# Chunk 0's k and q as bf16 over the software queue, chunk 2's x turned by the DMA engines: a fused window attention and MLP kernel

## The chip, the core and the metric

The kernel runs on one core of one Trainium2 chip. The metric is the device time of one execution in microseconds (us); the number shown is the median of three runs. The engines are named as in the profile: PE is TensorE's matmul side and PEld its weight loads, DVE is VectorE, ACT ScalarE, POOL GpSimd, SP SyncE. POOL, SP and ACT can all issue DMAs. Those of POOL go through the software queue (q0 in the profile), which can change the type on the way; those of SP and ACT go through hardware queues (q1 and q10), which cannot, but which can transpose bf16 data. All share 16 DMA engines.

## The reference

Inputs are q, k and v of shape (4, 8, 768, 64) in fp32 (batch, heads, tokens, head size). Each query attends to the 128 latest keys and to the first 4 of its sequence; the result goes through a normalised MLP with a residual.

```python
scores = scale * np.matmul(q, k.transpose(0, 1, 3, 2))
keep = is_sink | in_window            # first 4 keys, or 0 <= i - j < 128
a = softmax(where(keep, scores, -1e9))
x = (a @ v)                           # heads side by side: (4, 768, 512)
xn = (x - mu) / np.sqrt(var + 1e-06) * g_ln
out = x + np.maximum(xn @ w_ch1, 0.0) @ w_ch2     # w_ch1 512 x 2048, w_ch2 2048 x 512
```

## The kernel before, in words

**Tiling.** The 4 x 768 tokens are 24 tiles of 128, or 12 chunks of 256; a sequence has three chunks. Chunks 0 to 2 are the first sequence. For each chunk, `chunk(c)` (L642) loads k, q and v and turns k and q so that the head size lies along the partitions; `attend_tile(t)` (L724, chunks 0 and 1), `attend(c)` (L784, chunk 2) or `block(t)` (L902, all later ones) computes scores, exponents and the product with v; `normalise` (L865) takes the mean and variance of x and subtracts the mean (tile `xc`); and `mlp(c)` (L1015) does the two big products. The second product's result is scaled by the inverse deviation when the residual is added (L1070), and stored by SP (L1074).

**Order.** The program has no loops at run time over this: each piece of work is an operation (`P.op`) with the engines that may do it, an estimated duration, a priority, and the buffers it reads and writes. `Plan.run` (L114) places them, before the program is built, on a model of the engines, of PSUM and SBUF slots and of the DMA engines, each engine taking among the operations that could start about now the one with the lowest priority number. The instructions are then written out in the order of the planned start, engine by engine; on the chip each engine works through its list in that order. A load's plan entry has three numbers: the time it keeps the DMA engines, the delay to its first byte, and the delay after its last. In the gaps that the plan shows on TensorE in the first 24 us, matmuls on a zeroed tile are put in (L1132).

**k and q of chunk 0 (L647 to L676).** They come in quarters: k and q, each in two halves of four heads. SP issues k's halves and ACT q's (L656), in fp32, into tile `natf`; a row of a partition holds two neighbouring tokens (i = 0, 1) of each head, so that one run of memory is 512 bytes. ACT or DVE casts each quarter to bf16 (L660, `natc`). Four matmuls against the identity turn it (L668): each has 128 partitions and two heads of 64 columns, and writes into a PSUM tile `one`, even tokens for i = 0 and odd ones for i = 1. One eviction of 512 columns (L639) copies it to `kT` or `qT`. `tile_of` notes which eviction the scores of a tile wait for: here one for both tiles.

**k and q of chunks 1 to 3 (`by_pairs`, L575).** POOL loads all eight heads in one load that casts to bf16 (L581, `natp`). Quarter matmuls of 64 partitions by 64 columns turn them (L596), and evictions (L639) put the tokens of each tile in order. From chunk 4 on (`by_dma=4`) k and q are loaded by POOL (L692, `nat`) and transposed by DMAs that SP issues (L573).

**x of a tile (L880 to L898).** For chunks below `x_by_dma` (3 before) TensorE transposes the four blocks of `xc` (L885), and an eviction (L896, DVE) multiplies by `g_ln` (tile `gt`) on the way to `xnt`, what the first product reads. From chunk `x_by_dma` on, SP issues a DMA transpose (L573 through `dma_t`), and `g_ln` must sit in w1 instead:

```python
        if c == PAR["x_by_dma"] - 1:
            for s in range(4):
                for j in range(NDM):
                    P.op(f"w1g{s}{j}", {"DVE": fix(0.26)}, 16.0 * c + 11.0 + 2 * s + 0.1 * j,
                         ... V.tensor_scalar_mul(w1[s][:, j, :], w1[s][:, j, :], gt[:, j:j + 1]) ...
                         reads=[Bw1[s], Bc["gt"]], writes=[Bw1g[s]], after=last_use[s])
```

So each of the four quarters of w1 is scaled in place on the DVE (L1096), once its last matmuls with the unscaled weights are done, and the first product of chunk `x_by_dma` waits for it.

**Other loads.** v of each tile (L616, later L634), w1 in four loads (L547) and w2 in four (L550) come through POOL, cast to bf16. The other set-up work: POOL makes the identity and the triangle mask (L467, L470), the DVE the masks and ones (L463 to L523), SP loads `gt` (L525) and the first four keys' v (L529).

**A second path.** If a sum of exponents is out of range, `general` (L236) computes everything again; it does not run here.

Of the kernel before, what the change touches and what calls it, by code (L numbers as in the profile page):

```python
# [65 lines left out]
class Plan:  # L66
# [47 lines left out]
    def run(self):  # L114
        free = {"PE": 0.9, "ACT": 0.75, "DVE": 0.9, "POOL": 1.3, "SP": 0.75}
# [81 lines left out]
def pe(us):  # L197
    return {"PE": (us, us + Plan.PE_DRAIN)}
# [17 lines left out]
HW_V = (0.2, 0.8, 1.2)  # L216
SW_P = (1.47, 0.7, 0.9)
# [14 lines left out]
PAR = dict(strict=400.0, win=0.4, tr=-8.0, sc=-5.0, sc1=-2.0, av=2.0, blk=-8.0, step=6.0, trx=9.0, by_dma=4, x_by_dma=3,  # L232
# [136 lines left out]
def kernel(  # L369
# [43 lines left out]
    ring("natc", 4, [128, 2, 4, 64], BF16)  # L413
# [197 lines left out]

    def load_v(t, prio):
        b, r = t // RB, t % RB
        bv = Buf(f"v{t}", "vn")
        vn_b[t] = bv
        P.op(f"vld{t}", {"POOL": (0.87, 0.9)}, prio, lambda e: G.dma_start(  # L616
            bv.t[:, :, 0:64], v[b, :, 128 * r:128 * (r + 1), :].rearrange("h p d -> p h d")),
            writes=[bv], dma=SW, after=list(ones_of.values()))
# [23 lines left out]
    def chunk(c):  # L642
# [3 lines left out]
        if c < 2:  # L646
            kT_b[c], qT_b[c] = Buf(f"kT{c}", "kT"), Buf(f"qT{c}", "qT")  # L647
            if c == 0:
                nats = [Buf("kf", "natf"), Buf("qf", "natf")]
                for hh in range(2):  # L650
                    hs = slice(4 * hh, 4 * hh + 4)
                    for i, (x, T) in enumerate(((k, kT_b[c]), (q, qT_b[c]))):
                        nm, src, part = "kq"[i], nats[i], Buf(f"{'kq'[i]}l{hh}")
                        ap = x[b, hs, 0:256, :].rearrange("h (p i) d -> p h (i d)", i=2)
                        P.op(f"{nm}ld{hh}", {("SP" if i == 0 else "ACT"): (0.53, 0.53)}, -70 + hh,
                             lambda e, src=src, ap=ap, hs=hs: (nc.sync if e == "SP" else nc.scalar).dma_start(  # L656
                                 src.t[:, hs].rearrange("p h i d -> p h (i d)"), ap), writes=[src, part], dma=HW_F)
                        nat, pt, done = Buf(f"{nm}c{hh}", "natc"), Buf(f"pt{nm}{hh}", "one"), Buf(f"{nm}T0{hh}")
                        P.op(f"cast{nm}{hh}", {"DVE": dve(512), "ACT": act(512)}, d + 0.01 * hh,
                             lambda e, nat=nat, src=src, hs=hs: (nc.scalar.copy if e == "ACT" else V.tensor_copy)(  # L660
                                 nat.t, src.t[:, hs].rearrange("p h i d -> p i h d")),
                             reads=[part], hold=[src], writes=[nat])

                        def tr(e, pt=pt, nat=nat):
                            pb = pt.t.rearrange("p (h m i) -> p h m i", h=2, i=2)
                            for hp in range(2):
                                for i in range(2):
                                    nc.tensor.matmul(pb[:, hp, :, i], lhsT=nat.t[:, i, 2 * hp:2 * hp + 2, :], rhs=ident,  # L668
                                                     start=hp + i == 0, stop=True, skip_group_check=True)
                        o = P.op(f"tr{nm}{hh}", pe(0.3), d + 0.02 + 0.01 * hh, tr, reads=[nat, Bc["ident"]], hold=[T], writes=[pt])  # L670
                        trs[0], trs[1] = trs.get(0, [o]), [o]
                        evict(f"ev{nm}0{hh}", d + 0.05 + 0.01 * hh, 512,
                              lambda pt=pt: pt.t.rearrange("p (h c) -> p h c", h=2),
                              lambda T=T, hh=hh: T.t[:, 2 * hh:2 * hh + 2, :], [pt], [T, done], fp=True)
                        for t in range(2):
                            tile_of[nm, t, hh] = done  # L676
# [499 lines left out]
```

## Time and profile before

| | us |
|---|---|
| median of the runs shown (3; 217.49 to 218.28) | 217.88 |
| the profiled execution | 219.3 |
| its span, first to last instruction | 217.8 |
| PE busy | 207.1 (95%) |
| DVE busy | 117.7 (54%) |
| ACT busy | 106.1 (49%) |
| POOL busy | 111.7 (51%) |
| mean granted TensorE clock (share of full) | 0.995 |

| DMA queue | packets | MB |
|---|---|---|
| software (q0) | 69872 | 13.18 |
| hardware, SP (q1) | 33024 | 13.61 |
| hardware, ACT (q10) | 1056 | 0.52 |

How to read it: the busy time of an engine is an average over stages. The kernel has a start of some 23 us, in which the first loads come and the attention of the first four tiles goes through all engines, and then eleven stretches of some 16 us, one to a chunk, in which TensorE has work all the time. In the views below, times in us run from the first instruction of the span. A line of the timeline has start, duration, engine, source line, operation, output and inputs, sizes, the number of instructions merged, and in brackets how long the engine sat idle before and what ended that. A line of the chain has start, duration and what it was. The packet records of the trace give each DMA packet's queue, size and time, and the landing records the time at which a load's semaphore was complete.

### The profile page before, as it was taken

How to read it: one execution, taken by the hardware profiler on the slowest of the kernel's cores; microseconds unless marked ns; L12 is line 12 of the kernel's file. 1: busy time of each engine (PE TensorE's matmuls, PEld its weight loads, DVE VectorE, ACT ScalarE, POOL GpSimd, SP SyncE). 2: the span in 40 equal slices, each digit the busy share in tenths (PEclk: the TensorE clock that was granted, in tenths of full speed). 3: DMA queues.
4: the chain of work that ended last, by engine and by line, in shares of the span. 5: the costliest groups of instructions: out<-in, count | busy, mean ns of one | idle time of the engine just before them, and what ended most of it. 6: DMA issues, size and time to landing. Idle time of an engine off the chain costs nothing.

```text
span 217.8 us, 6716 instructions
## 1 busy us (share of the span) xinstructions
PE 207.1 (95%) x2774; PEld 145.3 (67%) x2797; DVE 117.7 (54%) x324; ACT 106.1 (49%) x171; POOL 111.7 (51%) x166
## 2 busy tenths in 40 slices
PE   6979999999999999999999999999999999999991
PEld 2657975765875875864865865865865866856760
DVE  5389874696986447446355456355366266262021
ACT  3687477155572562562562562552652652622600
POOL 7877642589961881871970980970960120120000
PEclk9999999999999999999999999999999999999998
DMA  5999999999999699799799799799999202203011
GB/s 155 171 188 204 194 206 193 181 132 136 204 161 125 115 127 146 83 194 147 110 148 139 110 137 157 107 142 144 113 142 138 75 1 74 72 7 116 0 54 60
DMA packets 103990, 27.82 MB, mean 128 GB/s; under 512 B 94224, under 2 KB 101008, under 8 KB 103952
## 3 DMA queue, kind: packets, MB, share of 16 engines
q0 software_dynamic: 69872, 13.18, 80.7%
q1 hardware_dynamic: 33024, 13.61, 32.5%
q10 hardware_dynamic: 1056, 0.52, 0.9%
q8 instruction: 24, 0.39, 0.8%
q14 instruction: 14, 0.11, 0.2%
HBM read 27.43 MB, written 6.29 MB: 155 GB/s over the span
## 4 chain that ended last, share of the span: by engine, by line
PE 90%; DVE 5%; issue 2%; ACT 1%; DVEq 0%
PE one L1062 38%; PE one L1033 35%; PE pair L967 3%; PE one L1026 2%; PE one L940 2%; PE pair L1132 2%; PE one L947 2%; DVE x L860 1%; PE one L956 1%; DVE st L868 1%; PE one L668 1%; PE one L975 1%; PE pair L740 1%; DVE xnt L896 1%; PE pair L596 1%
## 5 line engine op out<-in xcount | busy, mean ns | idle before, releaser
L1062 PE MATMUL one<-w,h 128*128 128x512 bf16 (+1 forms) x377 | 84.8, 370 | 2.3 <-issue 1.6
L1043 ACT ACTIVATE h<-one 128x512 bf16<-128x512 f32 x94 | 56.2, 598 | 48.6 <-PE one L1033 44.9
L1033 PE MATMUL one<-xnt,w 128*128 128x256 bf16 x704 | 79.5, 273 | 0.0
L1033 PEld LDWEIGHTS <-w 128*128 128x128 bf16 x704 | 68.5, 98 | 10.6 <-issue 0.3
L1062 PEld LDWEIGHTS <-h 128*128 128x128 bf16 x400 | 37.2, 98 | 39.1
L985 ACT ACTIVATE pe<-pair 128x768 bf16<-128x768 f32 x36 | 27.2, 808 | 43.0 <-PE pair L967 43.0
L634 POOL DMA_DIRECT2D vn<-in_v_dram x59 | 38.7, 701 | 9.9 <-DMA w<-in_moe_w_ch_dram 6.5
L877 POOL TENSOR_SCALAR st<-st 128x1 f32<-128x1 f32 x24 | 8.7, 363 | 66.7 <-DVE st L870 66.3
L1008 DVE RECIPROCAL rec<-one 128x4 f32<-128x4 f32 x36 | 6.4, 177 | 57.0 <-PE one L956 45.6
L1070 DVE SCALAR_TENSOR_TENSOR ot<-one,st,x 128x512 f32<-128x512 f32 (+1 forms) x25 | 18.2, 727 | 14.0 <-PE one L1062 9.3
L878 POOL TENSOR_TENSOR st<-st,mhalf 128x1 f32<-128x1 f32 x24 | 16.9, 703 | 2.0
L868 DVE BATCH_NORM_STATS2 st<-x 128x6 f32<-128x512 bf16 x24 | 16.7, 695 | 0.8
L1010 DVE TENSOR_TENSOR x<-one,rec 128x256 bf16<-128x256 f32 x36 | 15.3, 424 | 1.2
L692 POOL DMA_DIRECT2D nat<-in_k_dram x16 | 14.9, 939 | 1.1 <-DMA natp<-in_q_dram 1.1
L692 POOL DMA_DIRECT2D nat<-in_q_dram x16 | 14.3, 908 | 0.0
L990 DVE TENSOR_TENSOR pe<-pe,band 128x768 bf16<-128x768 bf16 x24 | 12.2, 551 | 0.0
L872 DVE TENSOR_SCALAR xc<-x,st 128x512 bf16<-128x512 bf16 x24 | 9.1, 381 | 1.1 <-DVE st L870 0.3
L967 PE MATMUL pair<-qT,kT 64*64 64x128 bf16 (+1 forms) x528 | 9.2, 204 | 0.0
L940 PEld LDWEIGHTS <-pe 128*128 128x128 bf16 (+1 forms) x144 | 6.2, 97 | 2.9 <-issue 0.8
L765 ACT ACTIVATE pe<-pair 128x1024 bf16<-128x1024 f32 (+1 forms) x8 | 7.1, 918 | 2.0 <-PE pair L759 1.0
L1026 PE MATMUL one<-xnt,w 128*128 128x128 bf16 x128 | 7.6, 219 | 0.0
L967 PEld LDWEIGHTS <-kT 64*64 64x64 bf16 x528 | 7.2, 108 | 0.4 <-issue 0.4
(106 smaller groups left out, 165.2 us busy)
## 6 DMA issues: line engine op xcount, KB each, us to landing
out_dram<-ot SPq DMA_DIRECT2D x23, 256.0 KB
w<-in_moe_w_ch_dram POOLq DMA_DIRECT2D x8, 512.0 KB, 14.2
nat<-in_k_dram POOLq DMA_DIRECT2D x16, 128.0 KB, 4.8
nat<-in_q_dram POOLq DMA_DIRECT2D x16, 128.0 KB, 5.5
vn<-in_v_dram POOLq DMA_DIRECT2D x44, 32.0 KB, 5.5
vn<-in_v_dram POOLq DMA_DIRECT2D x15, 64.0 KB, 5.1
natp<-in_k_dram POOLq DMA_DIRECT2D x3, 256.0 KB, 13.8
vn<-in_v_dram POOLq DMA_DIRECT2D x6, 128.0 KB, 11.8
```

The source lines that it names most:

```text
L634: P.op(f"vld{t}_{i}", {"POOL": (0.8, 0.85)}, prio + 0.001 * i, lambda e, p0=p0, n=n, hs=hs, src=src: G.dma_start(m.t[p0:p0 + n, hs, 0:64], ...
L692: lambda e, nat=nat, ap=ap: G.dma_start(nat.t, ap), writes=[nat], dma=SW, after=gate(c))
L868: P.op(f"bn{t}", {"DVE": fix(0.60)}, d + 0.12, lambda e: V.bn_stats(st.t[:, 8:14], x.t), reads=[x], writes=[st, mv])
L878: G.tensor_tensor(st.t[:, 16:17], st.t[:, 17:18], mhalf, op=ALU.pow)),
L967: nc.tensor.matmul(pps[u].t[64 * g:64 * g + 64, h2, col + c0:col + c0 + n], lhsT=kt.t[rs, hp, k0:k0 + 64], rhs=qT.t[rs, hp, q0:q0 + n], st ...
L985: nc.scalar.activation(pes[j].t.rearrange("p a b -> p (a b)")[:, 0:768].rearrange("p (a b) -> p a b", a=2), pps[j].t[:, :, 0:384], AF.Exp, ...
L990: V.tensor_mul(at_s, at_s, band[j] if r > 1 else edge[r][j].unsqueeze(1).to_broadcast([128, 4, 192]))
L1010: P.op(f"x{t - 1}{u}", {"DVE": dve(256)}, d + 0.051 + 0.002 * u, lambda e, u=u, rc=rc, pv=pv: V.tensor_tensor(x.t[:, 256 * u:256 * u + 256 ...
L1033: nc.tensor.matmul(ph.t[:, 256 * s:256 * s + 256], lhsT=w1[ht // 4][:, j, 128 * (ht % 4):128 * (ht % 4 + 1)], rhs=xnt.t[:, j, :], start=j ...
L1043: nc.scalar.activation(hb.t, ph.t, AF.Relu)
L1062: nc.tensor.matmul(pc.t[:, 0:wd], lhsT=(h1[2 * s + i].t[:, 128 * ii:128 * ii + 128] if by_tile else h1[ht // 2].t[:, 256 * (ht % 2) + 128 ...
L1070: V.scalar_tensor_tensor(ot.t[:, sl], in0=pc.t[:, 0:wd], scalar=st.t[:, 16:17], in1=x.t[:, sl], op0=ALU.mult, op1=ALU.add),
```

## The change

Two things change, and three constants of the planner with them.

1. For chunk 0, the new function `by_halves` takes the place of the code at L649 to L676. POOL issues the four quarters of k and q, which are cast to bf16 on the way into `natc`; there is no cast on ACT or DVE, and SP and ACT issue none of these loads. Sixteen quarter matmuls of 64 by 64 turn each quarter into two PSUM tiles, one for each tile of tokens, and each has its own eviction of 256 columns. `tile_of` now names, for each tile, its own eviction; the second tile's has a priority number larger by 0.4. The loads' priorities put the first two ahead of the identity mask on POOL and the others around the triangle mask.
2. `x_by_dma` goes from 3 to 2: x of chunk 2 (tiles 4 and 5) is transposed by DMAs, and w1 is scaled by `g_ln` after chunk 1's first product instead of chunk 2's.

```diff
-        free = {"PE": 0.9, "ACT": 0.75, "DVE": 0.9, "POOL": 1.3, "SP": 0.75}
+        free = {"PE": 0.9, "ACT": 0.75, "DVE": 0.9, "POOL": 1.0, "SP": 0.75}
...
+SW_F = (0.74, 1.1, 0.9)
...
-... by_dma=4, x_by_dma=3,
+... by_dma=4, x_by_dma=2,
...
-    ring("natc", 4, [128, 2, 4, 64], BF16)
+    ring("natc", 4, [128, 4, 2, 64], BF16)
...
+    def by_halves(nm, src, T, hh, i, d):
+        nat = Buf(f"{nm}c{hh}", "natc")
+        ap = src[0, 4 * hh:4 * hh + 4, 0:256, :].rearrange("h (p i) d -> p h (i d)", i=2)
+        P.op(f"{nm}ld0{hh}", {"POOL": (0.6, 0.63)}, (-101.0, -100.0, -98.5, -97.0)[2 * hh + i], lambda e: G.dma_start(
+            nat.t.rearrange("p h i d -> p h (i d)"), ap), writes=[nat], dma=SW_F)
+        pts = [Buf(f"pt{nm}{hh}{r}", "one") for r in range(2)]
+
+        def tr(e):
+            for a in range(2):
+                for u in range(2):
+                    for h2 in range(2):
+                        for r in range(2):
+                            rs, cs = slice(64 * r, 64 * r + 64), slice(64 * h2, 64 * h2 + 64)
+                            pb = pts[r].t[:, 0:256].rearrange("p (h i m) -> p h i m", h=2, i=2)
+                            nc.tensor.matmul(pb[cs, a, u, :], lhsT=nat.t[rs, 2 * a + h2, u, :], rhs=ident[rs, rs],
+                                             start=True, stop=True, skip_group_check=True)
+        o = P.op(f"tr{nm}0{hh}", pe(0.3), d + 0.02 + 0.01 * hh, tr, reads=[nat, Bc["ident"]], hold=[T], writes=pts, mode="q")
+        trs[0], trs[1] = trs.get(0, [o]), [o]
+        for r in range(2):
+            done = Buf(f"{nm}T0{hh}{r}")
+            evict(f"ev{nm}0{hh}{r}", d + 0.05 + 0.01 * hh + 0.4 * r, 256,
+                  lambda r=r: pts[r].t[:, 0:256].rearrange("p (h i m) -> p h m i", h=2, i=2),
+                  lambda r=r: T.t[:, 2 * hh:2 * hh + 2, 128 * r:128 * r + 128].rearrange("p h (m i) -> p h m i", i=2),
+                  [pts[r]], [T, done], fp=True)
+            tile_of[nm, r, hh] = done
...
-                        P.op(f"{nm}ld{hh}", {("SP" if i == 0 else "ACT"): (0.53, 0.53)}, -70 + hh,
...
-                        P.op(f"cast{nm}{hh}", {"DVE": dve(512), "ACT": act(512)}, d + 0.01 * hh,
...
-                        evict(f"ev{nm}0{hh}", d + 0.05 + 0.01 * hh, 512,
...
+                        by_halves("kq"[i], x, T, hh, i, d)
```

24 lines of the change are left out of this document (1 added, 23 removed).

## The prediction

> **What bounds the kernel now.** I read the chain of work that ended last, first its shares and then its pieces in time, then the timeline of the first 24 us, then the busy times by stage.
>
> ```profile
> PE 90%; DVE 5%; issue 2%; ACT 1%; DVEq 0%
> ```
> ```profile
> 8.01 0.59 ACT qT L639
> ...
> 8.94 0.54 PE one L668 x4
> ...
> 12.11 0.19 DVE rec L858
> ...
> 47.18 0.22 PE one L885 x4
> ...
> 48.27 0.22 PE one L885 x4
> ...
> 55.19 6.99 PE one L1033 x64
> ```
>
> TensorE sets the end: from about 23 us on its pieces follow each other without a hole, so a microsecond saved there, or by which that dense stretch starts earlier, is a microsecond of the whole. The DVE's 5% lie before 23 us, where the chain goes through the attention of the first four tiles. The timeline shows what that stretch waits for:
>
> ```profile
> 1.02 1.01 SPq L656 DMA_DIRECT2D natf<-in_k_dram  x2
> ...
> 1.85 1.12 POOL L581 DMA_DIRECT2D natp<-in_k_dram  x1
> ...
> 7.25 0.43 DVE L660 CAST natc<-natf 128x512 bf16<-128x512 f32 x1 [0.30 <-DMA natf<-in_q_dram]
> ...
> 8.87 0.61 PE L668 MATMUL one<-ident,natc 128*128 128x128 bf16 x4
> ...
> 9.48 0.74 POOL L547 DMA_DIRECT2D w<-in_moe_w_ch_dram  x1 [0.42 <-DMA natp<-in_k_dram]
> 9.52 0.69 DVE L639 CAST qT<-one 128x512 bf16<-128x512 f32 x1 [1.84 <-PE one L668]
> ```
> ```profile
> 12.00:15.00 3.00, 2.44 (x81) 1.76 (x77) 2.71 (x7) 2.69 (x5) 2.64 (x3) 1.00 1.62 187
> ...
> 21.00:24.00 3.00, 2.93 (x58) 2.65 (x56) 2.90 (x9) 1.19 (x2) 2.17 (x3) 1.00 1.34 201
> ```
>
> The last quarter of k and q lands at 7.22, is cast until 7.68, turned at 8.87, evicted until 10.21, scored at 10.36; the first reciprocal of tile 0 starts at 12.11. By stage (window, length, then busy us of PE, PEld, DVE, ACT, POOL) the DVE is nearly full from 12 to 24 us: once it has work, it is the bound until TensorE takes over.
>
> **The change, first half: k and q of chunk 0.**
> *Landing.* Four issues move from SP and ACT to POOL. POOL is free at 1.1 (its sequencer waits from 1.08). Each has 512 packets; the nearest rows with 512 are v loads (0.77) and weight loads (0.74): 0.75 each, 0.12 more for the first (1.12 against 0.9 to 1.0 for later ones of its form), and two mask instructions of 0.29 between them: the last ends at 1.1+3.0+0.12+0.58=4.8. When the software queue is idle, its first packet comes 1.69 us after the issue starts, 0.71 after it ends (72.67 to 74.36, again at 88.91 and 104.79). It moves 71 packets of 256 B per 0.1 us (packet records, 7.1 to 7.5 us), 0.72 a load; landing comes about 1.1 after the last packet (66.86 to 68.12). So the first lands near 1.1+1.69+0.72+0.3 (slow start)+1.1=4.9 and the last near 4.8+0.71+0.72+1.1=7.3. Before it was 4.86 and 7.22: nothing won or lost here. SP and ACT lose two issues of 0.5 each; what stood behind them, gt (used at 15.7) and the table load, is early anyway. POOL keeps eight loads under way (the 9.48 row waits for the first to land); with four more ahead each later load waits for the same one as now, so no wait is added.
> *From landing to scores.* Gone: four casts (0.61 on ACT twice, 0.43 on DVE twice). Sixteen quarter matmuls replace four whole ones: at L596, 32 of them start within 0.25 us and drain 0.19, so 16 take 0.3 (double that at the slow clock of the first 7 us, where 512 columns take 0.43 instead of 0.22). Evictions go by halves: about 0.35 instead of 0.69 for what tile 0 needs, and the second half can follow. The last quarter: 7.3+0.1+0.3=7.7 turned, 8.1 evicted, scores by 8.5, exponent (0.59) 9.1, value matmuls (0.42) 9.5. Tile 0's reciprocal comes at 9.5 instead of 12.1: 2.6 earlier.
> *What is late next.* The loads behind. Before, hardware packets of k and q moved until 6.4 and software packets began at 5.99, at full rate from 7.0. Afterwards the software queue is through k and q at 4.8+0.71+0.72=6.2 and goes on without a start. POOL issues the rest 3 us later than now, which that queue covers: the next issue ends near 5.7, before 6.2. So I leave the landings (the trace's records of each load's semaphore) where they are, within 0.5: v of tile 1 at 12.77, q of chunk 1 at 11.55, v of tile 2 at 16.31. Tile 1's value matmuls (13.29) can then gain 0.4 only; tile 2's scores (14.13) go to 11.55+0.5 turned+0.6 evicted+0.1=12.75, a gain of 1.4; tile 2's values (17.04) gain 0.5 in their first half; tile 3 depends on the DVE, which starts 2.6 earlier and pauses. The bounds are 0.4 and 2.6; I take 1.4, that of tile 2's scores, since half of what the DVE does until 24 us comes after them. Weights: w1's third and fourth quarter land at 22.09 and 24.68 and are used at about 23.9 and 26.0, w2's first at about 30.4 (its second at 32.98, less 2.55 a load) for 31.26. The margins are 1.8, 1.3 and 0.9, and where one is short, chunk 1's eight matmul groups (0.87 each) can go first.
>
> **Second half: x of chunk 2.**
> Two groups of transposes leave TensorE: 2 x 0.22=0.44 on the chain, where nothing else covers them. Two evictions of 0.69 leave the DVE. SP gets two transposes of 1.2 to 1.95 (row of the later ones); their 512 packets are out 1.3 to 4.7 us after the issue. xc is ready at 44.57 and 46.74, the user starts at 55.19: hidden. Behind them on SP wait two small copies (47.23) and chunk 4's k and q, due at 62. While such a transpose moves 111 packets per 0.1 us (59.1 to 59.3) the software queue moves none, so POOL's loads lose 0.5 twice, also for chunk 4.
> The scaling of w1 (16 x 0.346=5.5 us of DVE, now 57.1 to 62.8) must now lie between chunk 1's last use of each quarter (about 30.5 to 45.6) and 55.19, and chunk 2's first matmuls wait for it.
>
> ```profile
> 36.00:42.00 6.00, 5.95 (x66) 3.80 (x57) 2.99 (x5) 2.54 (x3) 2.94 (x5) 1.00 1.96 173
> 42.00:48.00 6.00, 5.84 (x126) 4.63 (x124) 5.70 (x14) 3.25 (x6) 4.33 (x8) 1.00 1.32 155
> 48.00:54.00 6.00, 5.79 (x96) 3.05 (x96) 4.05 (x11) 2.45 (x5) 6.00 (x9) 1.00 1.88 130
> ```
> The third busy time is the DVE's. Two quarters (2.8) fit before 42, where 3.0 of 6 are free; the others (2.8) into 42 to 54, where 0.3+1.95+1.38 (the evictions that go)=3.6 are free. Cost 0; without that cover TensorE would wait for one quarter, up to 1.4.
>
> **Sum.** 1.4+0.44=1.85. The profiled execution took 219.3 us, its span 217.8 and 1.5 around it; it becomes 217.45. The median of the runs shown is 217.88, so I predict 216.0.
>
> **Rivals.**
> *The software queue starts late (slower).* The only row of a first software load is natp: issued at 1.85, first packet at 5.99, 4.14 later instead of 1.69. I took the hardware queues for the reason: they move 65 packets of 512 B per 0.1 us until about 6.0, software packets rise as theirs fall, and 59.1 to 59.3 shows a hardware transfer shutting software out. If instead the queue needs that time by itself, k's first packet comes at 5.2, the four loads' packets end at 5.2+0.5+2.88=8.6 and q lands at 9.7. All behind them is then 8.6 against 6.5, 2.1 late: v of tile 1 at 14.9, its values at 15.0 instead of 13.3 (1.7 lost), w1's last quarter at 26.8 for 26.0. With the 0.44 back: +1.25, 219.1. It decides from a first packet of k later than about 3.9.
> The Trainium skill (DMA: Bandwidth & Descriptors, section on queues, rings and completion order) has each DMA engine go round between its queues packet by packet, which speaks for this rival; beside an output store at 58.0 us the trace agrees (15 packets of each queue per 0.1 us), beside the transpose at 59.1 it does not.
> *The DVE's set-up holds the descriptors (slower).* It is 88 to 99% busy from 1 to 4 us and ends at 4.2; 4.2 and the idle queue's 1.69 give 5.9, near the 5.99 seen. Then k's first packet stays there, 0.8 later than in the rival above: about 219.5. Against it: POOL's issues beside that work take 1.12 and 0.91, hardly more than 0.88 later.
> The Trainium skill (SBUF — State Buffer, section on its two separate sides) says that GpSimd cannot write descriptors while a two-port DVE operation holds their shared port, and advises the hardware queue; no run here shows it apart.
> *The gain stops at the weights.* If the order does not fill the margins of 0.9 to 1.8, or tile 1's v holds the whole DVE row (0.4), and the w1 scaling costs a few tenths, some 0.3 to 0.5 is left: 217.5.
>
> **How the numbers follow.** Forecast 0.55 (own range 215.2 to 217.1); more, up to the 2.6 of tile 0, 0.05 (214.8); weights 0.13 (217.5); late queue 0.19 (219.1); set-up 0.08 (219.5). A measurement of this kernel tells about 0.3%, 0.65 us, from no change: the third rival is "same". Faster 0.60, same 0.13, slower 0.27. The range must reach into the slow cases: 214.8 to 219.3.
>
> **What would show it.** Right: k's first software packet near 2.8, the last load landed near 7.3, the first reciprocal near 9.5, tile 2's scores near 12.8, and 0.4 less between 46 and 50 us, with no wait before chunk 2's first group. Wrong: a first packet at 4 or later, weights that the first groups wait for, or a DVE row that still ends at 27.

## The result, and the profile after

The changed kernel takes 220.32 us (median of six runs, 218.89 to 220.82) where the kernel before takes 218.41 (six runs, 217.49 to 218.99): the ratio is 1.0082, with a 95% interval of 1.0055 to 1.0109. It is slower by 1.9 us. The forecast was 216.0, its range ended at 219.3. The profiled execution took 220.82, its span 219.2, at a granted clock of 0.996 (before: 219.3, 217.8, 0.995).

The chain of the changed kernel, its shares first and then its pieces in time (start, duration, what):

```profile
PE 80%; DMA 13%; POOL 3%; issue 2%; DVE 0%; POOLq 0%; DVEq 0%
```
```profile
1.55 0.45 POOL natc L616
...
4.69 0.70 POOL natc L616
...
6.50 1.69 POOL natp L582 x2
...
9.10 8.36 DMA w<-in_moe_w_ch_dram
17.46 0.29 issue
17.75 14.47 DMA w<-in_moe_w_ch_dram
...
32.27 0.39 PE one L1064
```

Before, the first 23 us of this chain were the attention of the first tiles, on ACT, PE and DVE. Now they are POOL, which issues one load after another, and the weights that come last in that list: TensorE's second product starts at 32.27, 0.05 after the first quarter of w2 has landed (32.22). Two starts before it follow a landing as closely: 18.52 after v of tile 2 (18.48) and 26.87 after the fourth quarter of w1 (26.82). In the kernel before, these three loads land 0.7 to 1.3 us ahead of their use. The DVE has gone from the chain (5% to 0%).

The timeline has the steps that the prediction named (start, duration, engine, line, operation, and in brackets the idle time before it and what ended that):

```profile
1.55 0.96 POOL L616 DMA_DIRECT2D natc<-in_k_dram  x1 [0.82 <-POOLq L1159]
...
4.62 0.77 POOL L616 DMA_DIRECT2D natc<-in_q_dram  x1
5.38 1.13 POOL L643 DMA_DIRECT2D vn<-in_v_dram  x1
...
9.10 0.79 POOL L548 DMA_DIRECT2D w<-in_moe_w_ch_dram  x1
```
```profile
8.20 0.43 PE L627 MATMUL one<-ident,natc 64*64 64x64 bf16 x16 [1.09 <-DMA natc<-in_k_dram]
```
```profile
9.49 0.42 DVE L666 CAST qT<-one 128x256 bf16<-128x256 f32 x1
11.46 0.18 DVE L860 RECIPROCAL rec<-one 128x4 f32<-128x4 f32 x1 [1.55 <-PE one L847]
```

By the landing records the quarters of k and q land at 4.96, 5.80, 8.15 and 8.90. The first is where the forecast had it (4.9), the last is 1.6 later than forecast (7.3), and tile 0's first reciprocal comes at 11.46: 0.65 earlier than before, not 2.6. What decides the result is behind them:

| load (landing, us) | before | after | later by |
|---|---|---|---|
| natp, q of chunk 1 | 11.55 | 13.04 | 1.5 |
| v of tile 2 | 16.31 | 18.48 | 2.2 |
| w1, second quarter | 19.55 | 21.70 | 2.15 |
| w1, fourth quarter | 24.68 | 26.82 | 2.1 |
| w2, second quarter | 32.98 | 34.81 | 1.8 |

The chain's list of longest pieces has chunk 2's 64 first-product matmuls at 55.19 before; after:

```profile
56.18 6.99 PE one L1035 x64
```

That is 0.99 later, and 1.33 by 121 us. The stages that the prediction showed (window, length, busy us of PE, PEld, DVE, ACT, POOL):

```profile
12.00:15.00 3.00, 2.61 (x84) 1.49 (x83) 2.45 (x7) 2.10 (x5) 3.00 (x5) 1.00 1.60 187
21.00:24.00 3.00, 2.91 (x58) 2.71 (x56) 2.88 (x7) 1.59 (x3) 2.67 (x6) 1.00 1.23 202
...
42.00:48.00 6.00, 5.84 (x131) 4.73 (x131) 5.62 (x13) 2.61 (x5) 3.99 (x8) 1.00 1.54 184
48.00:54.00 6.00, 5.55 (x47) 2.54 (x47) 5.09 (x15) 2.81 (x6) 5.92 (x9) 1.00 1.59 133
```

From 12 to 15 us POOL is full (3.00, 2.64 before) and the DVE has idle time (2.45, 2.71 before). From 48 to 54 TensorE has 5.55 where it had 5.79, although the eight transposes are gone: part of the missing time is a wait, which the timeline of 46 to 54 us shows on DVE and then PE:

```profile
48.26 2.88 DVE L1098 TENSOR_SCALAR w<-w,gt 128x512 bf16<-128x512 bf16 x8
51.06 0.33 DVE L703 COPY kts<-kT 64x16 bf16<-64x16 bf16 x2
```
```profile
51.45 0.24 PE L977 MATMUL one<-qT,kts 128*32 128x64 bf16 x8 [0.40 <-DVE kts L703]
```

The two quarters of w1 that are scaled last stand ahead of the copy of the first keys, `kts`, which stood at 48.31 before.

**TensorE is slow for longer.** Two products of 512 columns that add the mask (`pair<-neg,ident`) have the same form in both kernels. Before and then after:

```profile
9.28 0.64 PE L740 MATMUL pair<-neg,ident 128*128 128x512 bf16 x2
```
```profile
9.30 1.04 PE L742 MATMUL pair<-neg,ident 128*128 128x512 bf16 x2
...
13.68 0.60 PE L742 MATMUL pair<-neg,ident 128*128 128x512 bf16 x2
```

By the trace's clock records TensorE has full speed for good from 7.47 us before and from 12.88 us after (until the last 2 us). In the six executions with k and q of chunk 0 by the hardware queues and no spare loads it is from 5.6 to 7.8 us, in the four whose start is the changed kernel's from 11.8 to 17.4. The prediction counted on full speed after 7 us. No run was made to set this apart from the late loads, but two of those below show a size: kts_first and loads_only start with the same work; q of chunk 1 lands at 13.52 and 13.57 and v of tile 2 at 18.27 and 18.24, but full speed comes at 13.07 and 17.43, and chunk 0's first product starts at 19.48 and 20.41. So a part of what the experiments give to the loads can be this clock; how large a part is open.

**Where the loads lost their time.** The DMA view of the first 20 us, GB/s in slices of 0.5 us, before and then after:

```profile
GB/s 0 0 0 0 78 82 266 333 342 330 287 283 127 127 171 165 158 158 164 177 171 169 182 189 202 209 201 181 171 158 172 214 186 199 201 207 205 209 201 215
DMA packets 10436, 3.55 MB, mean 177 GB/s; under 512 B 7024, under 2 KB 10435, under 8 KB 10435
```
```profile
GB/s 0 0 0 0 2 2 27 61 177 172 122 36 148 161 161 70 106 142 130 148 179 168 168 171 159 154 175 202 207 227 192 165 155 161 175 197 208 205 209 203
DMA packets 10091, 2.67 MB, mean 134 GB/s; under 512 B 9066, under 2 KB 10090, under 8 KB 10090
```

The seventh to twelfth number are 3 to 6 us. Before, the hardware queues bring k and q in fp32 there, at 307 GB/s on average (packets of 512 B). Afterwards these slices hold 99: the software queue starts at 3.21, its packets are of 256 B, and in its fullest slices it moves 160 to 180. (The view counts the bytes that are written. A packet of k or q carries 128 numbers in either kernel, as fp32 in 512 B and as bf16 in 256 B.) In the first 20 us the kernel before moves 3.55 MB, 1.05 of them k and q in fp32 (four loads of 256 KB); the changed one moves 2.67, 0.52 of them k and q in bf16. All other loads have 2.50 MB behind them in the one and 2.15 in the other. The 0.35 MB that lack are 1.75 us at the 200 GB/s of the last slices: the delays of the table once more, in bytes.

### The profile page after: what moved, and what is told of

The parts are those of the page before. It is cut to its first block, busy times and chain, and to the rows that moved or that the text cites. A ratio compares the mean times of both kernels' runs of the same rounds, so it can differ in the third digit from the quotient of the medians.

```text
span 219.2 us, 6791 instructions
## 1 busy us (share of the span) xinstructions
PE 206.8 (94%) x2811; PEld 143.6 (65%) x2834; DVE 114.2 (52%) x321; ACT 105.5 (48%) x172; POOL 114.6 (52%) x170
## 3 DMA queue, kind: packets, MB, share of 16 engines
HBM read 27.43 MB, written 6.29 MB: 154 GB/s over the span
## 4 chain that ended last, share of the span: by engine, by line
PE 80%; DMA 13%; POOL 3%; issue 2%; DVE 0%; POOLq 0%; DVEq 0%
PE one L1064 36%; PE one L1035 34%; DMA w<-in_moe_w_ch_dram 10%; PE pair L969 3%; DMA xnt<-xc 2%; PE one L942 2%; PE one L949 2%; POOL natc L616 1%; PE one L958 1%; PE one L977 1%; POOL natp L582 1%; POOL vn L643 1%; PE pair L847 0%; PE pair L721 0%; PE pair L597 0%
## 5 line engine op out<-in xcount | busy, mean ns | idle before, releaser
L879 POOL TENSOR_SCALAR st<-st 128x1 f32<-128x1 f32 x24 | 9.2, 384 | 62.3 <-DVE st L872 61.7
L880 POOL TENSOR_TENSOR st<-st,mhalf 128x1 f32<-128x1 f32 x24 | 16.4, 683 | 2.0
```

The source lines that it names most:

```text
L880: G.tensor_tensor(st.t[:, 16:17], st.t[:, 17:18], mhalf, op=ALU.pow)),
```

## The experiments

Twelve runs of eleven kernels. **Theory A**: the whole loss is in the loads' half, because four loads now stand on the one queue that carries all else, ahead of all else; and the x half gains nothing because w1's scaling stands ahead of `kts`. The rivals are in the expectations. Times of one kernel differ from run to run by 1.5 to 2 us (218.89 to 220.82 above). A part of that lies behind the last piece of work: from the end of the last eviction (`ot` on the DVE) to the end of the span it is 2.8 to 4.3 us, and 2.9 and 4.3 in two executions of one kernel, hw_quarters. So a term of 0.3 us is looked for in the trace, and the table has the end of that eviction; it too differs by 0.5 between those two.

| kernel | ratio to before [95%] | first software packet | natp q landed | w2's 2nd quarter landed | chunk 2's first products | last eviction ends |
|---|---|---|---|---|---|---|
| before | 1 | 5.99 | 11.55 | 32.98 | 55.19 | 213.79 |
| changed | 1.0082 [1.0055, 1.0109] | 3.21 | 13.04 | 34.81 | 56.18 | 215.11 |
| x_only | 1.0002 [0.9973, 1.0031] | 6.28 | | 32.98 | 55.41 | 214.34 |
| loads_only | 1.0073 [1.0044, 1.0102] | 3.22 | 13.57 | 34.99 | 56.63 | 215.23 |
| spare_loads | 1.0105 [1.0067, 1.0143] | 6.22 | 14.66 | 36.26 | 58.14 | 216.74 |
| hw_quarters | 0.9977 [0.9950, 1.0003] | 6.26 | | 33.50 | 54.85 | 213.45 |
| kts_first | 1.0097 [1.0058, 1.0136] | 3.22 | 13.52 | 34.62 | 55.69 | 214.33 |
| masks_first | 1.0071 [1.0047, 1.0095] | 3.54 | 13.62 | 35.44 | 57.14 | 215.74 |
| k_by_sp | 1.0023 [0.9996, 1.0050] | 3.89 | 11.82 | 33.38 | 55.23 | 213.83 |
| hw_both | 0.9991 [0.9964, 1.0018] | 6.29 | 11.87 | 33.28 | 54.65 | 213.26 |
| spare_hw | one run, 220.13 us | 5.96 | | 35.31 | 57.24 | 215.84 |
| x_own_copy | 0.9938 [0.9912, 0.9964] | 6.20 | 11.74 | | 54.20 | 213.54 |
| hw_quarters_again | 0.9980 [0.9961, 0.9998] | 6.16 | 11.67 | 33.01 | 54.35 | 212.95 |
| after_own_copy | 1.0069 [1.0039, 1.0100] | 3.22 | | 34.70 | 55.60 | 214.20 |

An empty cell is a load whose landing no record gives. The last five columns are those of one profiled execution each.

### x_only: the x half alone

```diff
-... by_dma=4, x_by_dma=3,
+... by_dma=4, x_by_dma=2,
```


> The kernel before with x of chunk 2 turned by DMA transposes and nothing else changed (the computation is whole). Theory A (the loss of the change comes from the loads that stand behind k and q in the software queue: w1's and w2's quarters land some 2 us later and TensorE waits for them; the x half only loses its gain of 0.44 us to a wait for the kts copy, which stands on the DVE behind the scaling of w1): 218.1 to 218.6 against 218.4, with a wait of 0.3 to 0.5 us for kts near 49 us. Rival B (the x half keeps its gain, all the loss is elsewhere): 217.9 to 218.0 and no wait. Rival C (the x half is what costs): 219 or more.

218.65 us, 1.0002: no change. Its chain holds the reason, and its timeline the wait:

```profile
47.17 2.72 DVE w L1096 x8
```
```profile
50.67 0.24 PE L975 MATMUL one<-qT,kts 128*32 128x64 bf16 x8 [0.54 <-DVE kts L701]
```

The 0.44 us of transposes are gone, and TensorE waits 0.54 for `kts`; at chunk 3 (71.82) it waits 0.17 for a DMA transpose of x, which it did not before. By the interval of the time the x half neither brings nor costs more than 0.7 us; in this execution the last eviction ends 0.55 later.

### loads_only: the first chunk's loads alone

```diff
-... by_dma=4, x_by_dma=2,
+... by_dma=4, x_by_dma=3,
```
(against the changed kernel)

> The changed kernel with x_by_dma back at 3 (the computation is whole): k and q of chunk 0 by the software queue alone. Theory A: the whole loss is here, 219.7 to 220.6 against 218.4, with w1's second quarter landing near 21.7 us and w2's first near 32.2. Rival C: within 0.3 of 218.4.

220.00 us, 1.0073: the loss is here. In its profiled execution the chain leaves POOL at another load:

```profile
7.37 6.20 DMA natp<-in_q_dram
```

q of chunk 1 lands at 13.57, two us later than before, and from there the chain goes through the DVE's work for the first four tiles; the first w2 quarter lands at 32.45 and is used at 32.66. In the changed kernel's profiled execution the weights led, here chunk 1's q does; both are late by 1.5 to 2.0 us in either execution. TensorE is slow until 17.43 here, and its pieces of this chain take longer for it (0.97 at 14.26 for two mask products that took 0.59 before).

### spare_loads: the same four loads, added to the kernel before, read by nobody

```diff
+    for i in range(4):
+        spare = const(f"spare{i}", [128, 4, 2, 64], BF16)
+        P.op(f"spare{i}", {"POOL": (0.001, 0.001)}, -97.0 + 0.1 * i, lambda e, i=i, t=spare: G.dma_start(
+            t.rearrange("p h i d -> p h (i d)"), (k, q)[i % 2][0, 4 * (i // 2):4 * (i // 2) + 4, 0:256, :].rearrange("h (p i) d -> p h (i d)", i=2)),
+            dma=(0.0, 0.0, 0.01))
```


> The kernel before with four additional software loads of 512 packets each (the same quarters of k and q, cast to bf16, into spare tiles that nothing reads) on POOL ahead of natp; k and q of chunk 0 themselves still come by the hardware queues, and the order of every other instruction on every engine is that of before (the result is whole). It sets the lateness of the loads behind apart from the lateness of k and q. Theory A: w1's second quarter lands 2 to 3 us later than its 19.55, and the kernel is slower by 1.0 to 2.0: 219.4 to 220.4. Rival D (what costs is that the later quarters of k and q land 1.7 us later and the attention of the first tiles with them): 218.2 to 218.7, since those are as before.

221.22 us, 1.0105: more than the whole loss, with k and q where they were. The spare loads land at 8.01, 8.86, 9.72 and 10.65, 0.88 us apart, and chunk 1's k, the next in the list, at 12.77 instead of 9.19:

```profile
1.90 3.13 POOL spare L559 x4
5.04 7.73 DMA natp<-in_k_dram
```

So four loads of 512 packets ahead of the others cost 3.6 us there and 2.8 to 3.6 at the weights. The changed kernel pays less (1.5 to 2.2); its queue starts 3 us sooner, with no fp32 loads beside it, and spare_hw below measures what that is worth. Late k and q are not needed for the loss: here the last of them lands at 7.00. TensorE has nothing to do from 10 to 12 us and runs at a granted clock of 0.50 from 12.29 to 19.12, so the loss here is that of late loads and slow clock together.

### hw_quarters, and again: the quarter matmuls and half evictions without the loads

The loads and casts of the kernel before stay; only the turning is new.

```diff
-    ring("natc", 4, [128, 2, 4, 64], BF16)
+    ring("natc", 4, [128, 4, 2, 64], BF16)
...
-                                 nat.t, src.t[:, hs].rearrange("p h i d -> p i h d")),
+                                 nat.t, src.t[:, hs]),
...
+                        pts = [Buf(f"pt{nm}{hh}{r}", "one") for r in range(2)]
...
+                                            nc.tensor.matmul(pb[cs, a, u, :], lhsT=nat.t[rs, 2 * a + h2, u, :], rhs=ident[rs, rs],
+                                                             start=True, stop=True, skip_group_check=True)
```


> The kernel before, its hardware loads and casts kept, with the changed kernel's quarter matmuls and its evictions by halves (the computation is whole): the turning alone, without the change of queue. Theory A: the first tiles' scores come some 1 to 2 us earlier, but v of tile 1, q of chunk 1 and the weights land as before and cap what is kept: 217.4 to 218.3. Rival D (the first chain sets the end): the gain goes through, 216.5 to 217.2.

> The kernel before with only the quarter matmuls and half evictions on its hardware loads and casts, once more beside the one with the x half and own copies, on the same chip. Theory A: ratio to the kernel before 0.996 to 0.999, as 0.9977 was, and above that of the kernel with own copies by 0.001 to 0.003; rival G: equal to it within 0.001; rival H (0.9977 was scatter, the quarter matmuls bring nothing): 0.999 to 1.001.

217.75 us (0.9977) and, run again, 218.44 (0.9980 [0.9961, 0.9998]): a small gain, told from no change the second time only. The loads land as before, and tile 0's reciprocal comes at 10.77 instead of 12.11: the turning does speed up the scores. But of those 1.3 us only 0.3 (54.85) and 0.8 (54.35) are left at chunk 2. The chain of the first of the two says why:

```profile
17.00 16.50 DMA w<-in_moe_w_ch_dram
```

w2's quarter, issued at 17.00 and landed at 33.50, is what the second product now waits for. That is the prediction's third rival, on a kernel that it was not written for: an earlier score chain runs into the weights.

### kts_first: w1's scaling later in the list

```diff
-                    P.op(f"w1g{s}{j}", {"DVE": fix(0.26)}, 16.0 * c + 11.0 + 2 * s + 0.1 * j,
+                    P.op(f"w1g{s}{j}", {"DVE": fix(0.26)}, 16.0 * c + 19.0 + 2 * s + 0.1 * j,
```


> The changed kernel, the scaling of w1 with a priority number larger by 8, so that the copy of kts stands ahead of it on the DVE (the computation is whole). Theory A: the wait of 0.40 us for kts near 51 us goes, and with it 0.3 to 0.5 us of the time: 219.2 to 220.0 beside 219.8 to 220.3 of the changed kernel in this call's terms (ratio to before 1.004 to 1.007). Rival C (the DMA transposes of x themselves cost): no change, 1.008.

The timeline shows the exchange, and no wait for `kts`; chunk 2 starts at 55.69 instead of 56.18:

```profile
48.49 0.34 DVE L703 COPY kts<-kT 64x16 bf16<-64x16 bf16 x2
48.87 3.11 DVE L1098 TENSOR_SCALAR w<-w,gt 128x512 bf16<-128x512 bf16 x8
```

The time, 220.33 us, is the changed kernel's (220.32). In the trace it keeps its lead (the last eviction ends 0.78 earlier), but the six runs do not have it. The expected gain in time did not come.

### masks_first: the four loads behind the two mask instructions on POOL

```diff
-        free = {... "POOL": 1.0, ...}
+        free = {... "POOL": 1.3, ...}
...
-        P.op(f"{nm}ld0{hh}", {"POOL": (0.6, 0.63)}, (-101.0, -100.0, -98.5, -97.0)[2 * hh + i], ...
+        P.op(f"{nm}ld0{hh}", {"POOL": (0.6, 0.63)}, (-97.8, -97.6, -97.4, -97.2)[2 * hh + i], ...
```


> The changed kernel with the two mask instructions of POOL ahead of the four loads instead of between them (the computation is whole). Theory A': the loads behind are paced by POOL's issues, and the two holes between them (0.3 us each) go: the fourth load's issue ends near 5.0 instead of 5.39, the loads behind come 0.3 to 0.6 us earlier, ratio to before 1.003 to 1.007. Rival E (the DVE's making of masks, which now falls beside the first two issues, holds their descriptors back): the first software packet comes at 4.2 us or later instead of 3.5, the loads behind as late as in the changed kernel or later, ratio 1.008 to 1.013.

220.14 us, 1.0071. The four issues now follow each other from 1.86 to 5.09 (0.97, 0.78, 0.77, 0.78 long) and end 0.3 earlier, and the DVE makes its masks between 2.28 and 4.02, beside the first three. The third quarter lands at 7.84 instead of 8.15 and tile 0's reciprocal comes at 10.93 instead of 11.46. Yet q of chunk 1 lands at 13.62, and its profiled execution has that on the chain ("6.79 6.83 DMA natp<-in_q_dram"). The order on POOL was not the cause. The three issues beside the DVE's work took as long as in the changed kernel (0.96, 0.78, 0.77), and the first packet came 1.68 after its issue, which speaks against the set-up rival too. TensorE runs at a granted clock of 0.50 from 10.40 to 17.23, which the expectation did not count on.

### k_by_sp: k back on SP, q on the software queue

```diff
+        if nm == "k":
+            raw = Buf(f"kf{hh}", "natf")
+            P.op(f"{nm}ld0{hh}", {"SP": (0.53, 0.53)}, -70 + hh, lambda e: nc.sync.dma_start(
+                raw.t[:, hs].rearrange("p h i d -> p h (i d)"), ap), writes=[raw], dma=HW_F)
+            P.op(f"castk{hh}", {"DVE": dve(512), "ACT": act(512)}, d + 0.01 * hh,
+                 lambda e: (nc.scalar.copy if e == "ACT" else V.tensor_copy)(nat.t, raw.t[:, hs]), reads=[raw], writes=[nat])
```


> The changed kernel with k's two quarters by SP's hardware queue in fp32 and cast, q's by POOL's software queue (the computation is whole). Theory A: half the additional software loads, half the lateness: natp's q lands near 12.3 (11.55 before, 13.04 changed), w1's second quarter near 20.6 (19.55 and 21.70), ratio to before 1.002 to 1.005. Rival D (the quarters of k and q in the first chain set the time): as k's second quarter lands earlier than 8.15, most of the loss goes, ratio 0.999 to 1.002.

219.13 us, 1.0023, with the x half in it. Two loads less on the queue, and q of chunk 1 lands at 11.82 (13.04 with four, 11.55 with none), w2's second quarter at 33.38 (34.81; 32.98). Tile 0's reciprocal comes at 9.15, the earliest of all kernels here: the forecast's 9.5 was possible, with both queues at work and TensorE at full speed from 4.47 on. It still waits 0.8 for `kts`. Most of the loss goes when half of the loads go; how much of that is the loads behind, and how much the clock, this run does not tell.

### hw_both: the quarters without the loads, and the x half with the scaling behind kts

```diff
-... by_dma=4, x_by_dma=3,
+... by_dma=4, x_by_dma=2,
...
-                    P.op(f"w1g{s}{j}", {"DVE": fix(0.26)}, 16.0 * c + 11.0 + 2 * s + 0.1 * j,
+                    P.op(f"w1g{s}{j}", {"DVE": fix(0.26)}, 16.0 * c + 19.0 + 2 * s + 0.1 * j,
```
(against hw_quarters)

> The kernel before with quarter matmuls and evictions by halves on hardware loads (as hw_quarters), with x of chunk 2 turned by DMA transposes and the scaling of w1 behind the copy of kts (the computation is whole): the two parts of the change that theory A holds to be gains, without the change of queue. Theory A: 0.5 from the first, 0.44 from the second: ratio to before 0.994 to 0.997. Rival: the weights, already waited for in hw_quarters (0.4 and 0.3 us), take the second gain too: 0.997 to 1.0.

218.39 us, 0.9991: the gain of theory A did not come here either; the rival's range has it. TensorE waits 0.8 and 0.2 for quarters of w1 and w2 (0.4 and 0.3 in hw_quarters). The chain shows another part:

```profile
47.71 2.51 DVE w L1102 x6
50.23 0.70 DVE w L1102 x2
50.93 0.94 DVE pe L996 x2
```

Behind `kts`, the eight scalings stand ahead of the next masks (`pe`, L996), and TensorE waits 0.3 for those. Wherever they stand between 47 and 51 us, something behind them is late.

### spare_hw: four fp32 loads that nobody reads, added to the changed kernel

```diff
+    for i in range(4):
+        spare = const(f"spare{i}", [128, 4, 2, 64], FP32)
+        P.op(f"spare{i}", {("SP", "ACT")[i % 2]: (0.001, 0.001)}, -120.0 + i, lambda e, i=i, t=spare: (nc.sync if e == "SP" else nc.scalar).dma_start(
+            t.rearrange("p h i d -> p h (i d)"), (k, q)[i % 2][0, 4 * (i // 2):4 * (i // 2) + 4, 0:256, :].rearrange("h (p i) d -> p h (i d)", i=2)),
+            dma=(0.0, 0.0, 0.01))
```


> The changed kernel with four spare fp32 loads of k and q (the ones the kernel before had), two from SyncE and two from ScalarE, issued first; nothing reads them, all of the software queue's loads and their order are kept. It asks why the software queue began at 5.99 in the kernel before, 4.1 after its first issue, and at 3.21 in the changed one, 1.66 after it. Theory A (the hardware queues' fp32 packets keep the software queue's out until they are through): the first software packet moves from 3.2 to about 6 (5.99 and 6.26 in the kernels that have these loads, 3.89 where two of the four are left), k's and q's last landing from 8.9 to about 11.5, the second chunk's natp of q from 13.0 to about 15.5, and the time is 2 to 3.5 us above the changed kernel's 220.3. Rival F (each software load starts some 1.7 after its issue whatever the others do, and natp was late for a reason of its own): first packet stays at 3.2 to 3.5, natp of q within 0.7 of 13.0, time 220 to 221.

The first software packet moves from 3.21 to 5.96, though POOL issues at 1.55 as before. The chain and the DMA view:

```profile
1.55 6.38 DMA natc<-in_k_dram
```
```profile
GB/s 0 0 0 0 57 75 238 346 343 319 287 290 232 165 147 175 180 178 168 160 168 181 183 178 180 181 163 168 200 201 244 193 186 167 155 159 183 192 208 211
```

So fp32 loads on the hardware queues do hold the software queue's first packet, 4.1 to 4.4 us after its issue in every kernel that has four of them and 2.3 in the one with two (k_by_sp), against 1.66 with none. The prediction's reading of the 5.99 was right, and the late-queue and set-up rivals had the wrong cause: the DVE's set-up is that of the changed kernel. The price was smaller than expected: the last of k and q lands at 10.59 (11.5 expected, 8.90 in the changed kernel), w2's second quarter 0.5 later (35.31), chunk 2 starts 1.06 later and the last eviction ends 0.73 later. The one run took 220.13, as rival F had it, but its span ends only 2.8 us behind that eviction (4.1 in the changed kernel). So a start of the queue that is 2.75 us later costs 0.5 to 1.1 us, far less than 2.75.

### x_own_copy: the scaled quarters in buffers of their own

```diff
+    w1x = w1[:2] + [const(f"w1x_{c}", [128, NDM, 512], BF16) for c in range(2, 4)]
...
-                                         lhsT=w1[ht // 4][:, j, 128 * (ht % 4):128 * (ht % 4 + 1)],
+                                         lhsT=(w1 if c < PAR["x_by_dma"] else w1x)[ht // 4][:, j, 128 * (ht % 4):128 * (ht % 4 + 1)],
...
-                    P.op(f"w1g{s}{j}", {"DVE": fix(0.26)}, 16.0 * c + 19.0 + 2 * s + 0.1 * j,
-                         lambda e, s=s, j=j: V.tensor_scalar_mul(w1[s][:, j, :], w1[s][:, j, :], gt[:, j:j + 1]),
-                         reads=[Bw1[s], Bc["gt"]], writes=[Bw1g[s]], after=last_use[s])
+                    P.op(f"w1g{s}{j}", {"DVE": fix(0.26)}, 16.0 * c + (11.0 + 2 * s if s < 2 else 2.0 + s) + 0.1 * j,
+                         lambda e, s=s, j=j: V.tensor_scalar_mul(w1x[s][:, j, :], w1[s][:, j, :], gt[:, j:j + 1]),
+                         reads=[Bw1[s], Bc["gt"]], writes=[Bw1g[s]], after=last_use[s if s < 2 else 0])
```
(against hw_both)

> The kernel before with the quarter matmuls on its hardware loads and casts, and the x half, where the third and fourth quarter of the scaled first weights are written to buffers of their own, so that they need not wait for the second chunk's last use of the unscaled ones and fall in VectorE's holes at 30 to 40 us (four scalings took 1.13 to 1.15 us there) instead of ahead of the kts copy or of the next chunk's masks. Theory A (the x half's 0.44 us is real and was given back only by eight scalings that stood at 47 to 51 us on VectorE): no TensorE wait for kts or for a masked pe at 48 to 54 us, third chunk's first products at 54.2 to 54.5 instead of 54.65 (eight scalings behind kts) and 54.85 (no x half), ratio to the kernel before 0.994 to 0.998. Rival G (the eight transposes lay in time that TensorE loses anyway, so that their going brings nothing wherever the scalings stand): third chunk's first products stay at 54.6 to 54.9, ratio the same as that of the kernel with the quarter matmuls alone within 0.001.

217.53 us (seven runs, 216.63 to 218.50), 0.9938 [0.9912, 0.9964]: faster than both kernels. The scaling has moved into the DVE's idle time, and `kts` and the masks are on time:

```profile
29.64 2.40 DVE L1103 TENSOR_SCALAR w1x<-w,gt 128x512 bf16<-128x512 bf16 x8
...
47.41 0.34 DVE L708 COPY kts<-kT 64x16 bf16<-64x16 bf16 x2
49.50 1.26 DVE L997 TENSOR_TENSOR pe<-pe,edge 128x768 bf16<-128x768 bf16 x2 [1.75 <-ACT pe L992]
```

Against the quarters alone on the same chip it is 0.42% less (0.9938 and 0.9980; the two intervals just touch), where 0.44 us, or 0.2%, was expected. The traces have no such gain: chunk 2 starts at 54.20 instead of 54.35, but chunk 3 then waits 0.59 for a DMA transpose of x, and from there on this kernel is behind. Chunk 3's first products in x_own_copy and in hw_quarters_again:

```profile
71.03 2.23 PE L1040 MATMUL one<-xnt,w 128*128 128x256 bf16 x19 [0.59 <-DMA xnt<-xc]
```
```profile
70.43 2.78 PE L1039 MATMUL one<-xnt,w 128*128 128x256 bf16 x24
```

The last eviction ends at 213.54 against 212.95. The execution with the trace, 218.29, was one of the slower of the seven. So that the scaling no longer costs a wait is shown; that the covered x half gains is what the times say and the traces do not, and it stays open.

### after_own_copy: the same in the changed kernel

The diff is that of x_own_copy, against the changed kernel.

> The changed kernel with the third and fourth quarter of the scaled first weights in buffers of their own, so that no scaling stands ahead of the kts copy; k and q stay on the software queue. Theory A (two separate terms: late weights cost about 0.7% to 0.8%, and the x half is worth 0.2% to 0.4% once its scaling is covered): no TensorE wait for kts at 48 to 54 us, weights as late as in the changed kernel (w1's last quarter 26.6 to 27.0, the first w2 quarter 32.0 to 32.4), third chunk's first products at 55.4 to 55.8 instead of 56.18, ratio to the kernel before 1.003 to 1.006. Rival G (beside the late weights the x half is worth nothing, as the changed kernel with the kts copy first, 1.0097, would have it): 1.007 to 1.010.

220.09 us, 1.0069: between the two expectations, and not to be told from the changed kernel. The trace has what theory A asked for, no wait for `kts`, weights as late as in the changed kernel (w2's second quarter at 34.70) and chunk 2 at

```profile
55.60 6.99 PE one L1036 x64
```

0.58 sooner than in the changed kernel; the last eviction ends 0.91 sooner. The time shows 0.23. So the loads make the loss with and without the x half, and beside them what its placement is worth stays open: 0.1% by the times, 0.3 to 0.4% by the traces.

## Why the prediction was wrong

**The failed step: "So I leave the landings (the trace's records of each load's semaphore) where they are, within 0.5."** The three that it names came 1.3 to 2.2 later. Its terms, one by one:
- *"POOL is free at 1.1"*: its first issue starts at 1.55, the fourth ends at 5.39 (forecast 4.8).
- *"Afterwards the software queue is through k and q at 4.8+0.71+0.72=6.2 and goes on without a start."* This is the term that failed: the last of them lands at 8.90, which, less the 1.1 between last packet and landing, is 7.8. The four took 4.6 us from the first packet, not four times 0.72 (2.9). The rate of one full-speed stretch was taken for the whole start, but in its first 0.7 us the queue has 4 to 34 packets per 0.1 us, and between 5.3 and 5.9 us 4 to 27, not 71, although the third load's issue had ended at 4.38. What made that hole is open. The DVE makes masks at 4.73 to 6.03, and in masks_first, where it makes them earlier, the hole is gone; but there q of chunk 1 is no sooner and the time the same.
- *"POOL issues the rest 3 us later than now, which that queue covers"*: the cover held (the next issue ends at 6.51, ahead of 7.8), but it says only that the queue is never empty. All behind is late by the 1.6 us between 6.2 and 7.8, and by 0.6 more from w1's first quarter on (17.46 instead of 15.29), of which no run shows the reason. spare_loads measures what four such loads cost those behind them, 2.8 to 3.6 us; the earlier start of the queue gives a part back (0.2 to 0.6 by w1 and w2 in spare_hw, 0.6 to 1.5 by their landings against spare_loads).

**The gain of 1.4 in the scores.** It rested on that step. The mechanism is right: without the loads, hw_quarters has tile 0's reciprocal 1.3 sooner, and with half of them k_by_sp 3.0. In the changed kernel it is 0.65: of the 1.96 us that are missing to the 9.5, 1.6 are the late landing, and the rest fits TensorE's clock, as the mask products ahead of the last scores take 1.04 there. Chunk 0's first product starts at 19.69 instead of 19.11; before it TensorE waits 0.52 for v of tile 2. That TensorE would run at full speed after 7 us was taken over from the kernel before without a reason.

**The weights' margins** of 1.8, 1.3 and 0.9 were right as a measure. A delay of 1.8 to 2.15 uses them up: w2's first quarter is used 0.05 after it lands.

**The x half.** "0.44" left TensorE as forecast. "Cost 0" for the scaling was wrong by the 0.40 to 0.54 that TensorE waits for `kts`. The sum of busy shares from 42 to 54 us did have room for 2.8 us; the DVE's list did not, because it works in order and something needed at once stood behind. The bound of 1.4 held. Once the scaling really had a cover (x_own_copy), the wait for `kts` was gone. "Hidden" was right for the transposes of chunk 2; in x_only and x_own_copy it is chunk 3 that waits 0.17 and 0.59 for its own, and the prediction asked only about chunk 4's k and q behind them.

**The rivals.** The late software queue was to decide "from a first packet of k later than about 3.9". It came at 3.21, so that rival's condition did not hold, and its cause is disproved: the queue is late only beside the hardware queues' fp32 loads (spare_hw). What it said of the loads behind ("2.1 late") is what happened, by another way: k and q took too long in the queue ahead of them, not too late a start; that its size fits is luck. The set-up rival falls by the first packet at 3.21, and by spare_hw, which brings the 5.96 back with the DVE's set-up unchanged. The third rival, the weights, is right as a limit, but sat beside a gain that was not there.

The Trainium skill (DMA: Bandwidth & Descriptors, section on queues, rings and completion order) has each engine go round between its queues packet by packet. In spare_hw no such alternation is seen at the start: with software loads issued from 1.55 on, no software packet moves until 5.96, while the hardware queues carry up to 346 GB/s; whether the software queue had its packets ready by then no run shows. The Trainium skill (the same page, section of rules for kernel authors) says that spreading DMAs over the issuing engines brings no bandwidth and saves only issue time. Here it does move the end: with two of the four loads back on SP (k_by_sp) the ratio goes from 1.0082 to 1.0023, and w2's second quarter lands at 33.38 instead of 34.81.

**Sum.** Forecast: -1.4 - 0.44. Measured, by the ratios times 218.4: +1.8 for the whole change (0.0082), +1.6 for the loads alone (0.0073), 0.04 for the x half alone (0.0002).

## What to carry to other kernels

Before a load is moved to another queue, add up the packets that then stand in that queue ahead of each later load, at the rate that the queue has in that stage and not at its best, and compare with what the old queue carried in the same microseconds; the first landing tells nothing of the last. Check in the trace at what clock TensorE goes through the stage whose length is forecast. Room in an engine's busy share is no cover for work that is placed in order: look at what stands behind it, and give it data that are ready early (here a buffer of its own) if it should fall into an earlier hole. A half of a change that shows no difference in the time may hold a saving and a wait that cancel (here 0.44 less work on TensorE and 0.54 of waiting): look for both in its trace.

## What the hardware showed that I had not expected

- An idle software queue's first packet comes 1.66 us after its issue also at the very start of the program; with four fp32 loads of 256 KB on the hardware queues it comes 4.1 to 4.4 after, with two 2.3.
- Packets of 512 B over the hardware queues move at 283 to 346 GB/s in the slices from 3.5 to 6 us; packets of 256 B over the software queue alone at 180 at most. In packets the two are alike: 63 to 73 per 0.1 us from 3.2 to 4.7 us before, 61 to 73 from 4.0 to 5.2 us after, each with 128 numbers.
- Each software load of 512 packets put ahead costs the next one 0.88 us (the spacing of the spare landings), more than the 0.72 that packets at full rate would take.
- The same two products of 512 columns take 0.60 us at TensorE's full granted clock and 1.04 before it is granted; when it is granted for good differs by 5.7 us between four kernels that start alike (11.78, 12.88, 13.07 and 17.43).
- From the end of the last eviction to the end of the span it is 2.8 to 4.3 us, and 2.9 and 4.3 in two executions of the same kernel.
